# Attention and token/channel MLP on one core: the vector loads, the spread over partitions and some transposes of the first batches done in another way

## The chip, the cores and the metric

The kernel runs on one core of one Trainium2 chip. The metric is the device time of one execution in microseconds. The core has five engines that this text names: PE (TensorE, matrix products and transposes), DVE (VectorE), ACT (ScalarE), POOL (GpSimd) and SP (SyncE, which here only issues DMA transfers). Each engine works through its own list of instructions in a fixed order and waits on semaphores for the others. Data move between the main memory and the on-chip memory by DMA; transfers issued by SP and ACT are described by hardware, those issued by POOL by software (the page calls the queues hardware_dynamic and software_dynamic).

## The reference

Grouped-query attention, and then a residual MLP over tokens and channels with affine layers in place of normalisation. There are 8 batches, 16 query heads on 4 key heads, 384 positions, head size 64 (so 1024 channels).

```python
scores = scale * np.matmul(q, k.transpose(0, 1, 3, 2))      # k, v repeated 4 times over the heads
attn = softmax(scores)
x = np.matmul(attn, v)                                      # as (batch, 384, 1024)
a1 = alpha1 * x + beta1
tok = np.einsum('ts,bsd->btd', w_tok, a1)
u = x + lam * tok
a2 = alpha2 * u + beta2
ch = np.maximum(a2 @ w_ch1, 0.0) @ w_ch2                    # 1024 -> 4096 -> 1024
out = u + lam * ch
```

## The kernel before

The eight batches run one after the other through two stages. The *side* of a batch is everything up to a2: scores, exponentials, AV (attention times v, `av_piece`), the first affine layer, the token product (`tok`), and the transpose of a2 to channels-by-tokens (`a2_transpose`). The *main* part of a batch is the two channel products: `h` (line 408; 32 groups of 8 matmuls, the result goes through bias and relu on ACT or DVE into `hT`) and `ch` (line 435; 6 groups of 32 matmuls). The side of batch b+1 is woven into the main part of batch b: `side` returns a list of small steps, and the loop at the end hands them out by the share of main's matmuls already done. All instruction orders are fixed when the program is built; nothing is rearranged later.

The first batch has nothing to be woven into. Its side is written out by hand: 18 score steps (`scores(i)`), and the table `at` (lines 377 to 383) says what follows each of them. DVE and ACT instructions are issued along with the PE work that feeds them, in the same order. This first stage lasts from 0 to about 42 us; main of the first batch begins there with matmuls of line 152, which belong to chunks 0 and 1.

In it, scale vectors are wanted in three forms. alpha1 times lam (`g1`) is wanted along the free axis in all partitions: the rows lie as 8 rows of 128 in `rows_f`, `scale_rows` (line 512) multiplies alpha1 and beta1 by lam, and `spread_g1` (line 328) spreads each row to 128 partitions by fp32 matmuls with a column of the identity. For the other vectors, `split` (lines 520 to 524) makes a sum of three bf16 parts of each row, and `spread` (line 319) spreads them with bf16 matmuls that add the parts up. alpha2 and beta2 are also wanted with channels on partitions (`al2T`, `be2`): two DMA loads of single elements (line 486). `rows_r` (line 307) makes the sums of w_tok's rows, which with `fill_h` carry beta1 through the token product.

Transposes: in the first two batches k and q are turned by PE, in later ones by DMA (`flip_k`, `flip_q`, issued by SP at 85% of the batch before). The first batch's u is turned in fp32 by PE and scaled by alpha2 in ACT's copy (line 278). For batch 1 (`pe_flip`) a2 is turned by PE (line 288) and copied by ACT (line 291); for batches 2 to 7 SP issues a DMA transpose (line 282). SP also issues the output stores (line 442).

First-layer weights come in 16 chunks of 512 KB a batch, each of them for two groups of `h`, through a ring of five buffers (`load_w1`, line 128, issued by POOL once PE has read the chunk five before). The second-layer weights are loaded once, half of them after the first batch's inputs, and the rest in pieces between the chunks of the first batch (`load_w2`, line 133). All of these go through the software queue in their order of issue.

POOL's order at the start is: the q loads and w_tok, its own copy of v into bf16 (line 536, waits for v), two chunks, the copies of k's second half (line 101), three chunks, a copy of beta2 (line 542), then the inputs of batch 1.

Of the kernel before, what the change touches and what calls it, by code (L numbers as in the profile page):

```python
# [12 lines left out]
def kernel(  # L13
# [21 lines left out]
    nc = tc.nc  # L35
    f32 = mybir.dt.float32
# [3 lines left out]
    MUL = mybir.AluOpType.mult  # L40
    ADD = mybir.AluOpType.add

    B, Hq, S, D = q.shape
# [4 lines left out]
    P = 128  # L48
    NST = S // P
    NDT = DM // P  # L50
    NNT = DFF // P
    NDW = DM // 512
    NP = Hq // 2
# [3 lines left out]
    RING = 5  # L57
# [6 lines left out]
    psum = ST(tc.psum_pool(name="psum", bufs=2))  # L64
# [13 lines left out]
    wtokT = const.tile([P, NST, S], bf, tag="wtokT", name="wtokT")  # L78
# [79 lines left out]
    def side(b):  # L158
# [113 lines left out]
        def a2_transpose(p):  # L272
            if first:
                ps = psum.tile([P, NST, P], f32, tag="tp" if p % 2 else "av", name="ut", bufs=1)
                for tt in range(NST):
                    nc.tensor.matmul(out=ps[:, tt, :], lhsT=x[:, tt, cols(p)], rhs=ident_f, is_transpose=True,  # L276
                                     start=(tt == 0), stop=(tt == NST - 1), skip_group_check=True)
                nc.scalar.activation(out=a2T[:, p, :S], in_=ps.rearrange("p a b -> p (a b)"),
                                     func=mybir.ActivationFunctionType.Copy, scale=al2T[:, p:p + 1])
                return  # L280
            if not pe_flip:
                nc.sync.dma_start_transpose(
                    out=a2T[:, p, :S].rearrange("p (a s) -> p a s", a=NST),
                    in_=a2s[p].rearrange("p a d -> p (a d)"))
# [17 lines left out]


        def rows_r(tag):
            ps = psum.tile([P, S], f32, tag=tag, name="r", bufs=1)
            for st in range(NST):
                nc.tensor.matmul(out=ps[:32], lhsT=ones, rhs=wtokT[:, st, :], start=(st == 0),
                                 stop=(st == NST - 1))
            t = hTf[:32, 10240:10240 + S]
            nc.vector.tensor_copy(out=t, in_=ps[:32])  # L310
            nc.vector.scalar_tensor_tensor(out=R[:32], in0=t, scalar=masks[2], in1=ps[:32], op0=MUL, op1=ADD)


        def spread(ps_, vs, tag, eng="DVE"):
# [3 lines left out]
            for i, p in enumerate(ps_):  # L318
# [6 lines left out]
        def spread_g1(ps_, tag):  # L325
            ps = psum.tile([P, 4, P], f32, tag=tag, name="vec", bufs=1)
            for i, p in enumerate(ps_):
                nc.tensor.matmul(out=ps[:, i], lhsT=ident_f[:NP, p:p + 1].to_broadcast([NP, P]),
                                 rhs=rows_f[:NP, :P], start=True, stop=True)
            nc.vector.tensor_copy(out=g1[:, ps_[0] * P:(ps_[-1] + 1) * P], in_=ps.rearrange("p n d -> p (n d)"))  # L330

        us = []

# [50 lines left out]
        for i in range(18):  # L384
            add(scores, i)
            for f, *a in at.get(i, []):
# [61 lines left out]
    with tc.manual_schedule(engines=order):  # L448
# [9 lines left out]
        load_k(0, [0])  # L458

        hTf = hT.rearrange("p n s -> p (n s)")  # L460
        rows_f = hTf[:32, 9216:10240].bitcast(f32)
        rows_t = hTf[:32, 10240:11264].bitcast(f32)
        rows_b = hTf[:, 11264:11776]
# [4 lines left out]
        be2, al2T = stage[:, 2112:2120], stage[:, 2856:2864]  # L468
        ident_f = hTf[:, 11776:12032].bitcast(f32)
# [5 lines left out]
        sel = stage[:, 2852:2856].bitcast(bf)  # L475
        for t in (stage[:, 2120:2824], rows_b, sel):
            nc.vector.memset(t, 0.0)
        nc.sync.dma_start(out=vst, in_=v[0].rearrange("h (p st) d -> p h st d", st=NST))
# [31 lines left out]
        def scale_rows():  # L510
            r = rows_f[:, :2 * P].rearrange("p (v d) -> p v d", v=2)
            nc.vector.tensor_tensor(out=r, in0=r, in1=rows_f[:, None, 3 * P:].to_broadcast([32, 2, P]), op=MUL)


        def split(lo, hi, step=None):
# [94 lines left out]
```

## Time and profile before

| | |
|---|---|
| median of 3 runs | 815.74 us (813.95 to 815.9) |
| the profiled execution | 814.52 us, its span on the core 812.6 us |
| PE busy | 800.2 us (98%) |
| DVE, ACT, POOL busy | 342.9, 228.1, 179.1 us |
| granted PE clock, mean | 0.996 |
| software DMA queue | 83.28 MB, 82.2% of the 16 DMA engines' time |
| hardware DMA queue of SP | 28.00 MB, 14.1% |

A profile is one execution. Busy PE time is modelled from the starts of pipelined matmuls, so that "98%" says that PE seldom waits, not that it is at its peak. A row such as `L328 PE MATMUL vec<-hT` names the line, the engine, the operation, and what is written from what. The name `hT` also stands for the vectors' rows, and `stage` for v, q and w_tok of the first batch, since these lie in buffers that are used for something else later.

### The profile page before, as it was taken

How to read it: one execution, taken by the hardware profiler on the slowest of the kernel's cores; microseconds unless marked ns; L12 is line 12 of the kernel's file. 1: busy time of each engine (PE TensorE's matmuls, PEld its weight loads, DVE VectorE, ACT ScalarE, POOL GpSimd, SP SyncE). 2: the span in 40 equal slices, each digit the busy share in tenths (PEclk: the TensorE clock that was granted, in tenths of full speed). 3: DMA queues.
4: the chain of work that ended last, by engine and by line, in shares of the span. 5: the costliest groups of instructions: out<-in, count | busy, mean ns of one | idle time of the engine just before them, and what ended most of it. 6: DMA issues, size and time to landing. Idle time of an engine off the chain costs nothing.

```text
span 812.6 us, 14143 instructions
## 1 busy us (share of the span) xinstructions
PE 800.2 (98%) x6098; PEld 453.1 (56%) x6152; DVE 342.9 (42%) x663; ACT 228.1 (28%) x315; POOL 179.1 (22%) x234
## 2 busy tenths in 40 slices
PE   8999999999999999999999999999999999999997
PEld 4766555665456655566455654556555565456545
DVE  6654544244433444334452444424444344442122
ACT  5654421432113321233103331034211432102100
POOL 6144330324003330123301341022500321003000
PEclk8999999999999999999999999999999999999999
DMA  9999997999159992799847997499944999129611
GB/s 198 198 184 200 203 212 133 175 173 175 38 134 178 180 137 66 138 180 175 114 96 131 172 177 90 113 140 176 173 70 100 158 167 132 37 65 183 92 40 40
DMA packets 232111, 112.58 MB, mean 139 GB/s; under 512 B 81009, under 2 KB 225905, under 8 KB 232049
## 3 DMA queue, kind: packets, MB, share of 16 engines
q0 software_dynamic: 169200, 83.28, 82.2%
q1 hardware_dynamic: 62304, 28.00, 14.1%
q8 instruction: 48, 0.79, 0.4%
q10 hardware_dynamic: 544, 0.39, 0.2%
q14 instruction: 15, 0.11, 0.0%
HBM read 170.53 MB, written 12.58 MB: 225 GB/s over the span
## 4 chain that ended last, share of the span: by engine, by line
PE 93%; DVE 3%; DMA 2%; issue 1%; SPq 0%; ACT 0%; DVEq 0%
PE ch L435 41%; PE h L408 37%; PE av L237 4%; PE sc L202 4%; PE tok L259 4%; DMA w<-in_moe_w_ch_dram 2%; DMA hT<-in_moe_lam_dram 1%; DVE hT L418 1%; PE h L152 1%; DVE x L243 1%; DVE a1f L250 0%; DVE a L252 0%; PE ut L276 0%; SPq L481 0%; DVE hT L521 0%
## 5 line engine op out<-in xcount | busy, mean ns | idle before, releaser
L408 PE MATMUL h<-a2T,w 128*128 128x384 bf16 (+1 forms) x2016 | 349.7, 326 | 1.0 <-DVE hT L418 0.3
L435 PE MATMUL ch<-w,hT 128*128 128x512 bf16 (+2 forms) x1546 | 346.1, 370 | 4.4 <-issue 1.0
L408 PEld LDWEIGHTS <-w 128*128 128x128 bf16 x2016 | 189.3, 98 | 125.6 <-issue 8.7
L128 POOL DMA_DIRECT2D w<-in_moe_w_ch_dram x128 | 112.4, 878 | 544.4 <-PE h L408 502.7
L435 PEld LDWEIGHTS <-hT 128*128 128x128 bf16 x1600 | 146.1, 98 | 153.0 <-issue 5.8
L211 ACT ACTIVATE es<-sc 128x1024 bf16<-128x1024 f32 x126 | 123.4, 1021 | 283.4 <-PE sc L202 283.4
L418 DVE TENSOR_SCALAR hT<-h,bias 128x384 bf16<-128x384 f32 x128 | 79.0, 617 | 187.1 <-PE h L408 186.5
L416 ACT ACTIVATE hT<-h,bias 128x384 bf16<-128x384 f32 x128 | 74.3, 581 | 202.9 <-PE h L408 202.4
L440 DVE TENSOR_TENSOR o<-ch,vecs 128x512 f32<-128x512 f32 (+2 forms) x50 | 33.3, 667 | 91.1 <-PE ch L435 91.1
L266 DVE TENSOR_TENSOR x<-tok,x 128x384 f32<-128x384 f32 x64 | 35.5, 555 | 81.3 <-PE tok L259 78.5
L237 PEld LDWEIGHTS <-es 128*128 128x128 bf16 x1008 | 45.8, 97 | 20.5
L237 PE MATMUL av<-v,es 128*128 128x65 bf16 x1008 | 49.0, 193 | 0.0
L202 PE MATMUL sc<-qT,kT 64*128 64x384 bf16 (+2 forms) x576 | 46.2, 275 | 0.1
L259 PEld LDWEIGHTS <-wtokT 128*128 128x128 bf16 x576 | 37.8, 98 | 12.4 <-issue 0.6
L242 DVE RECIPROCAL rinv<-av 128x6 f32<-128x6 f32 x64 | 12.3, 193 | 72.6 <-PE av L237 72.5
L259 PE MATMUL tok<-a,wtokT 128*128 128x128 bf16 x504 | 37.3, 219 | 0.0
L243 DVE TENSOR_TENSOR x<-av,rinv 128x384 f32<-128x384 f32 x64 | 35.7, 557 | 2.2
L202 PEld LDWEIGHTS <-kT 64*128 64x128 bf16 x576 | 19.9, 94 | 28.6 <-issue 24.2
L441 DVE TENSOR_TENSOR o<-o,x 128x512 f32<-128x512 f32 (+2 forms) x50 | 33.5, 671 | 1.7
L270 DVE TENSOR_TENSOR a<-x,vecs 128x384 bf16<-128x384 f32 x56 | 31.8, 569 | 1.9
L252 DVE TENSOR_TENSOR a<-a1f,vecs 128x384 bf16<-128x384 f32 x56 | 31.2, 558 | 2.2
L250 DVE TENSOR_TENSOR a1f<-x,vecs 128x384 f32<-128x384 f32 x56 | 31.2, 558 | 1.9
(75 smaller groups left out, 206.0 us busy)
## 6 DMA issues: line engine op xcount, KB each, us to landing
w<-in_moe_w_ch_dram POOLq DMA_DIRECT2D x135, 512.0 KB, 7.8
out_dram<-o SPq DMA_DIRECT2D x47, 256.0 KB, 2.0
q_raw<-in_q_dram POOLq DMA_DIRECT2D x28, 192.0 KB, 7.1
kst<-in_k_dram SPq DMA_DIRECT2D x16, 192.0 KB, 2.9
w<-in_moe_w_ch_dram POOLq DMA_DIRECT2D x10, 256.0 KB, 12.0
w<-in_moe_w_ch_dram POOLq DMA_DIRECT2D x1, 2048.0 KB, 15.3
v<-in_v_dram POOLq DMA_DIRECT2D x21, 64.0 KB, 6.9
a2T<-a SPq DMA_TRANSPOSE x48, 3.2
```

Source lines behind the costliest of these rows:

```text
L128: nc.gpsimd.dma_start(out=t, in_=w1src[:, :, c * CW * P:(c + 1) * CW * P])
L202: nc.tensor.matmul(out=sc[:, hh, k % 4:k % 4 + n], lhsT=kT[r, sk, 2 * p // G, :], rhs=qT[r, p, st:st + n, :], start=True, stop=True)
L211: nc.scalar.activation(out=e, in_=sc, func=EXP, scale=scale_qk)
L237: nc.tensor.matmul(out=av[:, hh, sq, :], lhsT=ess[k // 4][:, m % 2, k % 4, :], rhs=vb[:, sk, hk, :], start=(sk == 0), stop=(sk == NST - 1))
L243: nc.vector.tensor_tensor(out=x[:, :, cols(p)].rearrange("p st (h d) -> p h st d", h=2), in0=av[:, :, :, :D], in1=rinv.to_broadcast([P, 2, ...
L259: nc.tensor.matmul(out=ps[:, tt, :], lhsT=wtokT[:, st, tt * P:(tt + 1) * P], rhs=a1s[p][:, st, :], start=(st == 0), stop=(st == NST - 1 an ...
L266: nc.vector.tensor_tensor(out=u, in0=ps, in1=u, op=ADD)
L408: nc.tensor.matmul(out=ps[:, :n], lhsT=w1[:, dt, j * P:(j + 1) * P], rhs=a2T[:, dt, :n], start=(dt == 0), stop=(dt == NDT - 1))
L416: nc.scalar.activation(out=hT[:, nt, :], in_=ps[:, :S], func=RELU, bias=c1)
L418: nc.vector.tensor_scalar(out=hT[:, nt, :], in0=ps[:, :S], scalar1=c1, scalar2=0.0, op0=ADD, op1=mybir.AluOpType.max)
L435: nc.tensor.matmul(out=ps[:, lo:hi], lhsT=hT[:, nt, ms * P:(ms + 1) * P], rhs=w2[:, nt, dw * 512 + lo:dw * 512 + hi], start=(nt == 0), sto ...
L441: nc.vector.tensor_tensor(out=o[:, lo:hi], in0=o[:, lo:hi], in1=x[:, ms, c], op=ADD)
```

## The change

- SP's loads at the start: alpha1 and lam now go ahead of v; beta1, alpha2 and beta2 follow after the second part of k, all as rows. The two loads of single elements are gone.
- alpha1 and beta1 are scaled by lam one at a time; alpha1 goes through `split` and the bf16 `spread` (`spread_g1` is gone), beta1's scaling and split come later, at step 6.
- alpha2 and beta2 are turned to channels on partitions by two small PE transposes within `rows_r`, and copied out by DVE. POOL's copy of beta2 is gone.
- The table `at` is laid out anew: the first AV comes after step 5 instead of step 4, most later ones and the token products one step later too; one warm-up matmul after step 3; `rows_r` after step 8.
- POOL issues all five weight chunks ahead of the copies of k's second half.
- Batch 1: the first six of its eight a2 transposes are DMA transposes issued by SP.

```diff
-            if not pe_flip:
+            if not pe_flip or p < 6:
                 nc.sync.dma_start_transpose(
                     out=a2T[:, p, :S].rearrange("p (a s) -> p a s", a=NST),
                     in_=a2s[p].rearrange("p a d -> p (a d)"))
...
         def rows_r(tag):
-            ps = psum.tile([P, S], f32, tag=tag, name="r", bufs=1)
+            ps = psum.tile([P, 512], f32, tag=tag, name="r", bufs=1)
...
+            turned = ps[:, S:S + 2 * NP].rearrange("p (i n) -> p i n", i=2)
+            for i, c in enumerate((2, 4)):
+                nc.tensor.matmul(out=turned[:, i], lhsT=rows_f[:NP, c * P:(c + 1) * P], rhs=ident_f[:NP, :NP],
+                                 is_transpose=True, start=True, stop=True, skip_group_check=True)
...
+            nc.vector.tensor_copy(out=al2T, in_=turned[:, 0])
+            nc.vector.tensor_copy(out=a2T[:, :, S:S + 1], in_=turned[:, 1, :, None])
...
-        at = {0: [(warmup, 3)], 1: [(k_transpose, 1, 1), (scale_rows,), (split, 1, 2, 0)],
-              2: [(q_transpose, 2, 2, "av"), (split, 1, 2, 1)],
-              3: [(spread_g1, lower, "tp")], 4: [(wtok_transpose, 0, "av"), (av, 0), (wtok_transpose, 1, "tp")],
-              5: [(wtok_transpose, 2, "av"), (fill_h, 0), (k_transpose, 2)], 6: [(av, 1), (rows_r, "av")],
-              7: [(q_transpose, 4, 2)], 8: [(av, 2), (fill_h, 4)], 9: [(spread_g1, upper, "tp")], 10: [(tok, 0), (av, 3)],
-              11: [(tok, 1), (q_transpose, 6, 2)], 12: [(ut, 0), (tok, 2)], 13: [(av, 4), (tok, 3)], 14: [(ut, 1), (ut, 2)],
-              15: [(av, 5), (ut, 3)], 16: [(tok, 4)], 17: [(av, 6), (tok, 5)]}
+        at = {0: [(warmup, 3)], 1: [(k_transpose, 1, 1), (scale_rows, 0), (split, 0, 1, 0)],
+              2: [(q_transpose, 2, 2, "av"), (split, 0, 1, 1)], 3: [(warmup, 1)],
+              4: [(spread, lower, (0, 1), "tp"), (wtok_transpose, 0, "av")], 5: [(av, 0), (wtok_transpose, 1, "tp")],
+              6: [(wtok_transpose, 2, "av"), (scale_rows, 1), (split, 1, 2), (k_transpose, 2)],
+              7: [(av, 1), (q_transpose, 4, 2, "av")], 8: [(rows_r, "tp"), (fill_h, 0)],
+              9: [(av, 2), (spread, upper, (0, 1), "av")], 10: [(q_transpose, 6, 2), (tok, 0), (fill_h, 4)],
+              11: [(av, 3)], 12: [(tok, 1), (ut, 0)], 13: [(av, 4), (tok, 2)], 14: [(ut, 1), (tok, 3)],
+              15: [(av, 5), (ut, 2)], 16: [(tok, 4), (ut, 3)], 17: [(av, 6), (tok, 5)]}
...
+        load_row(0, moe_alpha1)
+        load_row(3, moe_lam)
         nc.sync.dma_start(out=vst, in_=v[0].rearrange("h (p st) d -> p h st d", st=NST))
-
-        for i, ap in enumerate((moe_alpha1, moe_beta1, moe_alpha2, moe_lam)):
-            nc.sync.dma_start(out=rows_f[:, i * P:(i + 1) * P],
-                              in_=bass.AP(tensor=ap.tensor, offset=ap.offset, ap=[[0, 4], [P, NP], [1, P]]))
         load_k(0, [2])
-        with nc.allow_non_contiguous_dma(reason="one small vector, once"):
-            for t, ap in ((al2T, moe_alpha2), (be2, moe_beta2)):
-                nc.sync.dma_start(out=t, in_=ap.rearrange("(dt di) -> di dt", di=P))
+        load_row(1, moe_beta1)
+        load_row(2, moe_alpha2)
+        load_row(4, moe_beta2, 1)
...
-        load_w1(0)
-        load_w1(1)
+        for c in range(RING):
+            load_w1(c)
         place_k(0, 1)
-        for c in range(2, RING):
-            load_w1(c)
-        nc.gpsimd.tensor_copy(out=a2Ts[0][:, :, S:S + 1], in_=be2[:, :, None])
```

`load_row(i, ap, n=4)` loads a vector as 8 rows of 128 into columns i of `rows_f`, n times below each other.

More of the change, by code (lines that the diff above doesn't have):

```diff
@@ L304, in rows_r @@
         def rows_r(tag):
-            ps = psum.tile([P, S], f32, tag=tag, name="r", bufs=1)
+            ps = psum.tile([P, 512], f32, tag=tag, name="r", bufs=1)
             for st in range(NST):
-                nc.tensor.matmul(out=ps[:32], lhsT=ones, rhs=wtokT[:, st, :], start=(st == 0),
+                nc.tensor.matmul(out=ps[:32, :S], lhsT=ones, rhs=wtokT[:, st, :], start=(st == 0),
                                  stop=(st == NST - 1))
-            t = hTf[:32, 10240:10240 + S]
-            nc.vector.tensor_copy(out=t, in_=ps[:32])
-            nc.vector.scalar_tensor_tensor(out=R[:32], in0=t, scalar=masks[2], in1=ps[:32], op0=MUL, op1=ADD)
+            turned = ps[:, S:S + 2 * NP].rearrange("p (i n) -> p i n", i=2)
+            for i, c in enumerate((2, 4)):
+                nc.tensor.matmul(out=turned[:, i], lhsT=rows_f[:NP, c * P:(c + 1) * P], rhs=ident_f[:NP, :NP],
+                                 is_transpose=True, start=True, stop=True, skip_group_check=True)
+            t = hTf[:32, 10496:10496 + S]
+            nc.vector.tensor_copy(out=t, in_=ps[:32, :S])
+            nc.vector.scalar_tensor_tensor(out=R[:32], in0=t, scalar=masks[2], in1=ps[:32, :S], op0=MUL, op1=ADD)
+            nc.vector.tensor_copy(out=al2T, in_=turned[:, 0])
+            nc.vector.tensor_copy(out=a2T[:, :, S:S + 1], in_=turned[:, 1, :, None])
         def spread(ps_, vs, tag, eng="DVE"):
@@ L322, in spread @@
                       in_=ps[:, :n * w].rearrange("p (n v) d -> p n v d", n=n))
[L325 to L330, printed above, removed]
         us = []
@@ L460 @@
         hTf = hT.rearrange("p n s -> p (n s)")
-        rows_f = hTf[:32, 9216:10240].bitcast(f32)
-        rows_t = hTf[:32, 10240:11264].bitcast(f32)
-        rows_b = hTf[:, 11264:11776]
+        rows_f = hTf[:32, 9216:10496].bitcast(f32)
+        rows_t = hTf[:32, 10496:11520].bitcast(f32)
+        rows_b = hTf[:, 11520:12032]
         stage = sb.tile([P, NST * DM], f32, tag="x", name="stage", bufs=2)
@@ L467 @@
         wtok_in = stage[:, 1536:2112].bitcast(bf).rearrange("p (tt s) -> p tt s", tt=NST)
-        be2, al2T = stage[:, 2112:2120], stage[:, 2856:2864]
-        ident_f = hTf[:, 11776:12032].bitcast(f32)
+        al2T = stage[:, 2112:2112 + NDT]
+        ident_f = hTf[:, 12032:12288].bitcast(f32)
         R = stage[:, 2120:2312].bitcast(bf)
@@ L477, with load_row @@
             nc.vector.memset(t, 0.0)
+        def load_row(i, ap, n=4):
+            nc.sync.dma_start(out=rows_f[:n * NP, i * P:(i + 1) * P],
+                              in_=bass.AP(tensor=ap.tensor, offset=ap.offset, ap=[[0, n], [P, NP], [1, P]]))
+        load_row(0, moe_alpha1)
+        load_row(3, moe_lam)
         nc.sync.dma_start(out=vst, in_=v[0].rearrange("h (p st) d -> p h st d", st=NST))
-        for i, ap in enumerate((moe_alpha1, moe_beta1, moe_alpha2, moe_lam)):
-            nc.sync.dma_start(out=rows_f[:, i * P:(i + 1) * P],
-                              in_=bass.AP(tensor=ap.tensor, offset=ap.offset, ap=[[0, 4], [P, NP], [1, P]]))
         load_k(0, [2])
-        with nc.allow_non_contiguous_dma(reason="one small vector, once"):
-            for t, ap in ((al2T, moe_alpha2), (be2, moe_beta2)):
-                nc.sync.dma_start(out=t, in_=ap.rearrange("(dt di) -> di dt", di=P))
+        load_row(1, moe_beta1)
+        load_row(2, moe_alpha2)
+        load_row(4, moe_beta2, 1)
         for h in (0, 2):
@@ L507, with scale_rows @@
                 nc.vector.tensor_reduce(out=t[:n], in_=ident[:n, :n].rearrange("p (k c) -> p c k", c=NP), op=ADD, axis=AX)
-        def scale_rows():
-            r = rows_f[:, :2 * P].rearrange("p (v d) -> p v d", v=2)
-            nc.vector.tensor_tensor(out=r, in0=r, in1=rows_f[:, None, 3 * P:].to_broadcast([32, 2, P]), op=MUL)
+        def scale_rows(i):
+            r = rows_f[:, i * P:(i + 1) * P]
+            nc.vector.tensor_tensor(out=r, in0=r, in1=rows_f[:, 3 * P:4 * P], op=MUL)
         def split(lo, hi, step=None):
```

## The prediction

> **What bounds the kernel now.** I read the page first, then the chain, the tensor engine's waits, the stages, and the landing of each weight chunk.
>
> ```profile
> PE 800.2 (98%) x6098; PEld 453.1 (56%) x6152; DVE 342.9 (42%) x663; ACT 228.1 (28%) x315; POOL 179.1 (22%) x234
> ...
> DMA  9999997999159992799847997499944999129611
> ```
>
> TensorE is busy for 98% of the span, so a change pays only in PE work removed or in one of the few PE waits. The DMA row is full in the first slices, some 120 us. Part 4, the chain, in order of time:
>
> ```profile
> 3.98 5.84 DMA hT<-in_moe_lam_dram
> ...
> 73.09 13.36 DMA w<-in_moe_w_ch_dram
> 86.45 0.05 issue
> 86.50 1.48 PE h L408 x8
> ```
>
> The first line is the load that the change targets. The others tell more: the last first-layer weight chunk of the first batch (chunk 15) is issued at 73.09, lands at 86.45 and is used at 86.50. PE's waits in the first 100 us (total, times, longest):
>
> ```profile
> PE vec L328 <- PE sc L202: 0.9, 1, 0.9
> PE tp L188 <- DMA stage<-in_q_dram: 0.6, 1, 0.6
> PE tp L177 <- DVE wtokT L300: 0.4, 1, 0.4
> PE tp L297 <- DVE vecs L330: 0.3, 1, 0.3
> PE h L408 <- DVE hT L418: 0.3, 1, 0.3
> ```
>
> The 0.9 us is the fp32 spread; the chain puts lam and L512 behind it. The stages (PE busy with count, PEld, DVE, ACT, POOL, granted clock, DMA share, GB/s):
>
> ```profile
> 9.20:12.59 3.39, 2.50 (x37) 1.92 (x37) 2.50 (x8) 2.40 (x3) 1.51 (x3) 1.00 1.64 173
> 12.59:19.41 6.82, 6.14 (x57) 3.37 (x52) 5.52 (x15) 2.80 (x4) 5.27 (x8) 0.50 1.41 213
> 46.00:86.00 40.00, 39.63 (x346) 24.64 (x345) 20.04 (x47) 21.84 (x40) 18.42 (x24) 1.00 1.38 198
> 41.00:45.50 4.50, 4.48 (x33) 2.69 (x31) 2.71 (x9) 3.02 (x8) 1.97 (x3) 1.00 0.80 152
> 10.00:12.00 2.00, 1.53 (x15) 1.23 (x16) 1.90 (x6) 1.01 (x3) 0.92 (x3) 1.00 1.71 147
> 185.00:187.50 2.50, 2.50 (x25) 1.57 (x23) 1.82 (x4) 0.31 (x1) 0.88 (x1) 1.00 1.77 121
> ```
>
> PE runs at half clock from 12.59 to 19.41. From 46 to 86 the DMA engines carry 198 GB/s without a break, and PE loses its lead over the weights: chunk 5 lands at 48.9 and is used at 52.3 (lead 3.4 us), chunk 10 leads by 1.4, 13 by 1.1, 14 by 0.5, 15 by 0.05. A chunk with its second-layer piece takes 3.95 us to move, PE's work on it 3.2 to 3.5. So this stage is bound by DMA at its end: an earlier PE waits for chunk 15.
>
> **The Trainium skill.** "TensorE: Matmul & The Clock Gate", What's actually happening: the clock halves after an idle window of about 3.4 us, and windows run free of the kernel. The trace agrees on length (6.83 us, two windows), but it halved after a window 74% busy (2.50 of 3.39). "DMA: Bandwidth & Descriptors", Why small descriptors are slow: each packet has a fixed cost. Here the element loads of alpha2 and beta2 (2,048 packets of 4 bytes) fall into 10 to 12, where the rate is 147 against 195 just after. The same page, Issuing engines are not separate DMA queues: all transfers share 16 engines. The row 185.00 shows it: during one DMA transpose the rate falls to 121.
>
> **The change, part by part.**
>
> *First batch, early (7 to 42 us).* Removed: two fp32 spreads, 16 matmuls (8 in groups of 1.08 us), 2.16 us of PE. Added: two bf16 spreads at 0.22 (row L319, four of 128x128), one warm-up (0.17), and two small fp32 transposes, not in the trace: 0.06 each (floor, their moving side is 8 wide) to 0.14 (the ut row, 0.41 for three), I take 0.1. PE net: -2.16 + 0.44 + 0.17 + 0.20 = -1.35. On DVE the split of beta1 moves up from work with alpha1 to its own five instructions (0.21, 0.21, 0.34, 0.21, 0.40, 0.24 with its scale: about 1.7 us) ahead of the k copy, plus two 8-wide copies at 0.15 (row L414). SP issues alpha1 and lam second and third, so DVE's first scale waits for its k copy's end (8.74) rather than 9.95. v is issued at about 2.8 instead of 1.25: it landed 5.1 after its issue; at the same pace 7.9, with fewer bytes ahead 7.2. POOL waits there; five weight issues (0.88 each) now stand before the k copies, which end at about 7.2 + 0.83 + 4.4 + 0.96 = 13.4, against 12.04. k's transposes are due after 13.4 in both orders: covered by the second token-weight copy (L300). AV a step later covers v. Two new waits: SP holds alpha2's row until the first k load has landed (issued 0.74, DVE reads it at 4.12) and beta2's until alpha1's has; behind them stand only batch 1's k loads, not needed before 40. PE's two small transposes wait for these rows at about step 8 (18 us), where in the old order the element loads had landed by 15.4; behind them PE's scores, but the rows are 10 us early. ACT's scaled copies now wait for DVE's copy of alpha2 (about 20) rather than a DMA, and are first due at 25: hidden. POOL loses its wait of 0.8 us for beta2 and a copy (0.35, L542), ahead of batch 1's q loads, which have 15 us to spare: nothing.
>
> Laying DVE, ACT and PE rows end to end in the old order, with half clock in its place, gives 42.0 for the end of the early stage; the trace has 42.06. In the new order: 39.7 at full clock, 40.7 with the same half window. With v at 10: 40.9 and 42.1. So PE comes 1.3 to 2.4 us earlier to chunk 2.
>
> *What stops it.* The DMA stream up to chunk 15 has the same bytes. It gains (a) the element loads' cost: (195 - 147) x 2 / 195 = 0.5 us; (b) the dip at 41 to 45.5, which comes because chunk 5's load waits for PE to free chunk 0: (205 - 152) x 4.5 / 205 = 1.2 us, filled if PE is 1.2 us or more earlier. Sum 1.7.
>
> *Batch 1's flips.* Six of eight transposes leave PE: 3 matmuls, 0.17 us each in the chain; ACT loses six copies of 0.48 (L291), worth nothing, as ACT is 28% busy. One (86.11) is before chunk 15, where the wait swallows it; five after (95.3 to 125.4): 5 x 0.167 = 0.83 us gained. SP gains six DMA transposes:
>
> ```profile
> L282 SPq DMA_TRANSPOSE a2T<-a x48: 1177/1185/1832, 171.7 to 720.3; - x48
> ...
> DMA to landing us min/median/max: 2.3/3.2/7.5
> ```
>
> Each holds SP for 1.18 us, in the order p0, p1, out 1, p2, out 2, p3, out 3, p4, out 4, p5, the k and q flips of batch 2. Output stores behind them are 8 us apart, with four buffers. The q flip (issued 129.3, median landing 6.6, first needed at 140.84) has 4.9 us to spare; p5 costs it 1.2. Its q rows land at 126.5; four transposes at 1 us each less the 1.7 put that at 129. Hidden. The pieces of w2's second half land by 112.9, wanted from 118.3 on: hidden too.
>
> p0 isn't. It follows the first tok (77.4, DVE done 79.2) and moves 3 us later, while chunks 14 and 15 are in flight. Its price in a full stage: in 185.0 to 187.5 the software queue moved 413 packets, against 375/us in the quiet stretch before (5.0 us at 191 GB/s): 1.4 us lost; in 272.5 to 274, 349 packets: 0.6; in 175.5 to 178, 456: 1.1. I take 1.0.
>
> Chunk 15 lands 1.7 - 1.0 = 0.7 us earlier. Sum: 0.7 + 0.8 = **1.5 us gained**. From the profiled execution (814.52, span 812.6) that is 813.0; the median of the runs is 1.2 above it, so **814.2** against 815.74. About 0.3% (2.4 us) is what a measurement of this kernel can tell from no change: this lies inside.
>
> Bounds: gain (b) half reached and p0 at 1.4: 0.5 + 0.6 - 1.4 + 0.8 = 0.5. p0 at 0.6: 1.9; p0 outside the stage: 2.5.
>
> **Rivals.**
>
> *B: the early gain reaches the end.* If the transpose costs the weight queue little, or chunks come faster, 1.3 to 2.4 plus 0.83 to 1.0: 2.1 to 3.4, middle 2.8, so 812.9. For it: PE is on the chain nearly everywhere. Against: the lead of 0.05 us at chunk 15.
>
> *C: half clock in the paced stage (slower).* Waiting for chunks 13 to 15 makes PE 81% busy (3.2 of 3.95), and 74% was halved before. Place: 75 to 90. Price: 6.83 us at half is 3.4 lost, so one window ends at 814.2 + 3.4 = 817.6, inside 0.3%; from the second window on it decides: 817.6 + 3.4 = 821 less what the waits absorb (0.75 x 2), some 819.5. Against: dense matmuls fill these chunks; 46 to 86 ran at 1.00.
>
> *D: early stage not shorter.* v or the k copies come late (v at 10), PE reaches chunk 2 as before. Only the flips are left: 0.8, less up to 0.9 as p0 now delays chunk 15: 815 to 815.8.
>
> **Chances.** A (forecast) 0.55, B 0.22, C 0.11, D 0.12. A's own spread 812.9 to 815.7. Faster by over 0.3% (below 813.3): most of B and a tenth of A, 0.23; slower: C's upper part and scatter, 0.09; within: 0.68. Range 8 in 10: from B's middle and the scatter of the runs (1.95 us) 812.0, to C's first window 817.0.
>
> **What would show it.** The scale of alpha1 starts before 9 us; no fp32 spread; early stage ends at 39.5 to 41; no dip at 41 to 45; PE waits of 0.3 to 0.8 us for weight DMAs before chunks 12 to 15, chunk 15 used at about 85.8; p0's packets between 79 and 84 with the rate near 120; PE then without gaps, 0.83 us less work to 140. Wrong if chunk 15 is used before 84.8 (B), the clock shows 0.5 after 46 (C), the early stage ends after 41.7 (D), or the first scores of batch 2 wait for the q flip.

## The result and the profile after

The changed kernel takes 815.2 us (median of 4 runs, 814.74 to 817.27) beside 815.49 us for the kernel before (4 runs on the same chip): the ratio is 1.0005, interval 0.9983 to 1.0027. Measured again with 15 runs beside 43 (experiment e10), the ratio is 1.0017, interval 1.0008 to 1.0026, some 1.4 us more than before. The time lies in the range and within 0.3%, as forecast; but the gain of 1.5 us isn't there, and rival D (early stage not shorter) is what the trace shows. The profiled execution took 814.84 us with a span of 813.1, against 814.52 and 812.6.

The page of the changed kernel, the tensor engine's row and the row of the DMA engines' load:

```profile
PE 797.7 (98%) x6076; PEld 449.7 (55%) x6129; DVE 345.8 (43%) x671; ACT 225.2 (28%) x309; POOL 178.7 (22%) x233
...
DMA  9999999999169992799947997499945999129611
```

PE has 2.5 us less to do (797.7 against 800.2), and the time doesn't fall. The chain in order of time says what the work is waiting for instead (start, duration, what):

```profile
2.81 7.16 DMA stage<-in_v_dram
9.97 0.06 issue
10.03 0.90 POOL v L538
10.93 4.38 POOL w L128 x5
15.31 1.04 POOL k L101 x2
16.35 0.05 issue
16.40 0.51 PE tp L177 x6
...
73.16 0.72 issue
73.88 13.75 DMA w<-in_moe_w_ch_dram
87.68 1.48 PE h L407 x8
```

The chain used to begin with lam's row and DVE. Now it begins with v: its load, POOL's copy of it, POOL's five weight issues and k's copies stand in one row, and PE's transposes of k's second half wait at their end. Chunk 15 is still what PE waits for later: it lands at 87.63 and is used at 87.68, where before it was 86.45 and 86.50. PE's waits in the first 100 us (total, times, longest):

```profile
PE tp L177 <- POOL k L101: 2.7, 1, 2.7
PE warm L452 <- DVE wtokT L455: 1.5, 1, 1.5
PE vec L325 <- DVE hT L526: 0.8, 1, 0.8
PE tok L259 <- DVE x L266: 0.8, 2, 0.6
PE h L407 <- DMA w<-in_moe_w_ch_dram: 0.6, 1, 0.6
```

The wait of 0.9 us for the fp32 spread (L328) is gone, and 0.8 us at its successor L325 stands in its place: the bf16 spread waits for DVE's split. The first row is new, 2.7 us. POOL's timeline shows its cause; the brackets give POOL's idle time before the copy and what ended it, v's load:

```profile
10.03 0.90 POOL L538 CAST v<-stage 128x768 bf16<-128x768 f32 x1 [5.24 <-DMA stage<-in_v_dram]
10.88 4.43 POOL L128 DMA_DIRECT2D w<-in_moe_w_ch_dram  x5
15.26 1.08 POOL L101 CAST k<-kst 128x384 bf16<-128x384 f32 x2
```

The stages (window, length, PE busy with count, PEld, DVE, ACT, POOL, granted clock, DMA share, GB/s):

```profile
10.90:13.50 2.60, 2.13 (x39) 1.51 (x38) 1.87 (x6) 2.10 (x4) 2.60 (x4) 1.00 0.71 102
14.33:17.74 3.41, 1.34 (x29) 1.03 (x30) 3.01 (x9) 0.60 (x2) 3.41 (x6) 1.00 1.41 192
17.74:21.16 3.42, 3.42 (x29) 1.59 (x26) 2.43 (x6) 1.72 (x3) 2.05 (x4) 0.50 1.40 199
41.00:45.50 4.50, 4.49 (x29) 2.62 (x28) 2.78 (x10) 3.09 (x8) 1.75 (x2) 1.00 1.05 203
46.00:86.00 40.00, 39.69 (x348) 24.67 (x346) 20.05 (x48) 21.55 (x40) 19.13 (x24) 1.00 1.39 198
```

For the kernel before, the first of these windows:

```profile
10.90:13.50 2.60, 2.29 (x37) 1.65 (x37) 2.50 (x9) 1.09 (x2) 2.42 (x4) 0.82 1.58 176
```

Three things are to be seen. From 10.9 to 13.5 only 102 GB/s move, against 176: POOL waited for v until 10.03 and then copied it, the first weight chunk was issued at 10.88 instead of 7.16, and the weight queue ran dry. In the window 14.33 to 17.74 PE is busy for 1.34 of 3.41 us, and the next window runs at half clock. And the dip is gone from the stretch 41 to 45.5 (203 against 152 GB/s; from 42 to 46 it is 183 against 160), though the early stage ends later: chunk 2 is first used at 43.05, against 42.21. The stream is late by then, so that it still has work while PE frees the next buffer; e1 and e2 below test this reading from both sides.

The transposes that SP issues in batch 1 (duration on SP, then issue to landing):

```profile
L282 SPq DMA_TRANSPOSE a2T<-a x6: 1185/1236/1282, 80.0 to 128.0; - x6
...
DMA to landing us min/median/max: 6.2/6.8/7.3
```

From chunk 15's use to chunk 16's (the first of batch 1's main part) it takes 52.75 us instead of 53.59. So the account is: chunk 5 lands 0.51 us later (49.37 against 48.86), chunk 15 is used 1.18 later, chunk 16 0.34 later, and the execution takes 0.32 us longer. From the use of chunk 16 to the end it is 672.5 to 672.7 us in all fourteen traces of this study, so that the difference between two kernels is made before it.

### The profile page after: what moved, and what is told of

It is laid out like the page before. It is cut to its first block, busy times and chain, and to the rows that moved or that the text cites. A ratio compares the mean times of both kernels' runs of the same rounds, so it can differ in the third digit from the quotient of the medians.

```text
span 813.1 us, 14108 instructions
## 1 busy us (share of the span) xinstructions
PE 797.7 (98%) x6076; PEld 449.7 (55%) x6129; DVE 345.8 (43%) x671; ACT 225.2 (28%) x309; POOL 178.7 (22%) x233
## 4 chain that ended last, share of the span: by engine, by line
PE 92%; DVE 4%; DMA 3%; issue 1%; POOL 1%; SPq 0%; ACT 0%; DVEq 0%
PE ch L434 41%; PE h L407 37%; PE av L237 4%; PE sc L202 4%; PE tok L259 4%; DMA w<-in_moe_w_ch_dram 2%; DMA stage<-in_v_dram 1%; DVE hT L417 1%; DVE x L243 1%; PE h L152 1%; POOL w L128 1%; DVE a1f L250 0%; DVE a L252 0%; PE ut L276 0%; DVE rinv L242 0%
```

## The experiments

The theory after the result (V): v's late landing holds POOL, and through POOL both the weight queue and k's copies. Its rivals: the DMA transpose of block 0 takes the gain (called T in the expectations); the new order on PE and DVE is no shorter in itself (P); the delay is k's copies alone (an order on POOL, whatever v does); or it is PE's clock. Ratios are times against the kernel before, with 95% intervals; the kernel before had medians of 814.87, 814.66, 814.58 and 814.64 us in the four groups of runs (e1 to e4, e6 to e9, e10 to e12, e13).

### e1: v's load ahead of the rows again

```diff
+        nc.sync.dma_start(out=vst, in_=v[0].rearrange("h (p st) d -> p h st d", st=NST))
         load_row(0, moe_alpha1)
         load_row(3, moe_lam)
-        nc.sync.dma_start(out=vst, in_=v[0].rearrange("h (p st) d -> p h st d", st=NST))
```

> The changed kernel with v loaded ahead of the rows of alpha1 and lam again (one line moved). Theory V (v's late landing, at 9.97 us, costs the early gain twice: POOL's k copies come late and PE waits 2.7 us for them, and the weight queue, whose first chunk POOL issues after v's copy, runs dry from 11 to 13.5, so that every chunk lands later): v lands at 6.3 to 6.6, the first chunk is issued at about 7.3, PE's wait for the k copies is under 0.5 us, the early stage ends at 39.7 to 41, chunk 15 is used at 85.3 to 86.2, and the time is 1.5 to 2.3 us under the changed kernel. Theory T (the DMA transpose of batch 1's first a2 block, which moves while chunk 15 is in flight, sets the end by itself): chunk 15 is used within 0.4 us of 87.7 whatever the early stage does, time as the changed kernel. Theory P (the new order of PE and DVE is no shorter in itself): v lands early, but the early stage still ends at 42.5 or later.

Measured: 815.04 us, ratio 1.0006 (0.9995 to 1.0016). The means work: v lands at 6.39, the first chunk is issued at 7.21, k's copies are done at about 12.6, and the queue isn't dry. The windows of this kernel:

```profile
6.72:10.13 3.41, 3.41 (x21) 1.09 (x19) 0.77 (x2) 1.67 (x2) 3.41 (x5) 1.00 1.30 216
...
10.90:13.50 2.60, 1.53 (x16) 0.85 (x13) 2.02 (x7) 2.39 (x3) 2.60 (x5) 1.00 1.42 212
...
42.00:46.00 4.00, 3.98 (x30) 2.39 (x28) 2.30 (x7) 2.69 (x8) 1.80 (x3) 1.00 0.61 126
```

The end doesn't follow: the forecast of 1.5 us or more below the changed kernel is missed. What came is the sign named for theory P, and chunk 15 is used at 88.12, later than in the changed kernel. In this trace DVE's scale of alpha1 starts at 10.19 instead of 8.75, and the early stage ends at 42.88. In this execution that isn't the rows' later place: DVE waits for its k copy, and that one for PE, whose first products ran slower until 10.13 (0.61 us for a group of four score products that takes 0.39 afterwards; the record of the tensor clock begins with full speed at 10.13). In e11, which also has v first, the scale starts at 8.68. The groups on DVE of this kernel, from the copy to the end of the split:

```profile
9.91 0.36 DVE L179 COPY kT<-tp 128x384 bf16<-128x384 bf16 x1 [2.03 <-PE tp L177]
10.19 0.27 DVE L514 TENSOR_TENSOR hT<-hT 32x128 f32<-32x128 f32 x1
...
12.75 0.21 DVE L526 CAST hT<-hT 32x128 bf16<-32x128 f32 x1
```

So 2.8 us pass on DVE from the scale to the spread's operands, where the old spread needed the scale alone. The old early part, begun as slowly, loses nothing here: e12 (below) has its first full speed at 9.78, and its fp32 spread starts at 10.77 without a wait. The new one in e1, and the old one in e12 as far as the view goes (to 11 us):

```profile
13.02 0.38 PE L325 MATMUL vec<-hT,stage 128*128 128x128 bf16 x4 [0.79 <-DVE hT L526]
...
10.77 0.48 PE L328 MATMUL vec<-hT 8*128 8x128 f32 x2
```

A stream that is early and a PE that is late then give the deepest dip of all traces, 126 GB/s from 42 to 46. That explains this one execution. Whether the other twelve began as slowly isn't on record, so why e1 is no faster than the kernel before stays open.

### e2: k's copies after two chunks, as in the kernel before

```diff
-        for c in range(RING):
-            load_w1(c)
+        load_w1(0)
+        load_w1(1)
         place_k(0, 1)
+        for c in range(2, RING):
+            load_w1(c)
```

> The changed kernel with POOL's copies of k's second half ahead of weight chunks 2 to 4, as in the kernel before. v still lands late. If PE's 2.7 us wait for the k copies is what counts: time 1.5 us or more under the changed kernel. Theory V in full (the weight queue's delay counts as well): PE's wait falls to 0.5 us or less, the early stage ends about 1.5 us earlier (41.0 to 41.6), but chunk 15 still lands at 87.2 to 87.8, PE waits 1.5 to 2.5 us for chunks 12 to 15 instead of 0.6, and the time is within 0.4 us of the changed kernel.

Measured: 814.03 us, 0.9993 (0.9985 to 1.0002). PE's waits for k and for the weights:

```profile
PE tp L177 <- POOL k L101: 1.5, 1, 1.5
PE h L407 <- DMA w<-in_moe_w_ch_dram: 1.2, 1, 1.2
```

The early stage ends at 41.22, the queue is still dry (112 GB/s in 10.9 to 13.5), and chunk 15 is used at 86.40, not at the 87.2 to 87.8 that theory V in full named. The late stream meets an early PE, and what it lacked by 14 us it has again by 50 (see the table at the end):

```profile
42.00:46.00 4.00, 3.97 (x33) 2.52 (x30) 3.75 (x12) 1.56 (x5) 2.67 (x4) 1.00 1.27 241
```

So the place of k's copies is a part of the cost, the dry queue isn't needed for that part, and what a dry queue loses early need not be lost at the end.

### e3: block 0 of batch 1 turned by PE

```diff
-            if not pe_flip or p < 6:
+            if not pe_flip or 0 < p < 6:
```

> The changed kernel with blocks 1 to 5 of batch 1's a2 turned by DMA and block 0 by PE again. Theory T, and the price taken in the prediction: chunk 15 lands 0.6 to 1.0 us earlier (86.6 to 87.1), PE's wait of 0.6 us before it goes, and PE's transpose costs 0.17 back: time 0.3 to 0.5 us under the changed kernel. If block 0's transfer did not delay the chunk: chunk 15 lands at 87.6 as before, time the same.

Measured: 814.74 us, 1.0002 (0.9994 to 1.0010). In its profiled execution the wait for k's copies was 3.9 us, the early stage ended at 43.65 and one chunk interval was 4.74 us, so its trace doesn't compare with the other by the end (chunk 15 lands at 88.50, not at the forecast's 86.6 to 87.1). The interval from chunk 14's landing to chunk 15's does: 3.89 us, against 4.57. The DMA transpose is not where the gain went: without it the kernel is as fast as the kernel before, not faster.

### e4: the early part alone, batch 1 as before

```diff
-            if not pe_flip or p < 6:
+            if not pe_flip:
```

> The changed kernel with all of batch 1's a2 blocks turned by PE as in the kernel before: the early part of the change alone. As the prediction priced the flips: five transposes of 0.17 us come back after chunk 15, block 0's stands before it in place of 0.4 to 0.6 us of waiting; time 0.3 to 0.6 us over the changed kernel, 0.8 to 1.0 us over the kernel before, with chunk 15 used at 86.9 to 87.3.

Measured: 815.88 us, 1.0012 (1.0005 to 1.0020): the new early part costs 1.0 us by itself. The chain has the same head:

```profile
2.82 6.71 DMA stage<-in_v_dram
9.58 0.83 POOL v L538
10.41 4.34 POOL w L128 x5
14.75 1.06 POOL k L101 x2
```

### e6: two chunks ahead of POOL's copy of v

```diff
+        load_w1(0)
+        load_w1(1)
         nc.gpsimd.tensor_copy(out=vt[0][:, :, :, :D], in_=vst.rearrange("p h st d -> p st h d"))
-        for c in range(RING):
+        for c in range(2, RING):
             load_w1(c)
         place_k(0, 1)
```

> The changed kernel with weight chunks 0 and 1 issued by POOL ahead of v's copy (so they don't wait for v); the k copies still come after all five chunks. Theory V, its weight-queue half alone: the rate no longer falls between 11 and 13.5 (195 GB/s or more), the first half of w2 lands at 43.0 to 43.6 instead of 44.8, PE's wait for the k copies falls from 2.7 to about 0.9 us because only three issues stand ahead of them, the early stage ends near 41.2, the dip at 41 to 45 is gone, chunk 15 lands at 85.2 to 86.4; time 1.0 to 2.2 us under the changed kernel. If the queue running dry did not count: chunk 15 lands at 87 or later and the time stays within 0.5 us.

Measured: 813.95 us, 0.9989 (0.9983 to 0.9996). v is as late as in the changed kernel (landing at 9.70), but the queue is fed; k's copies are at 13.25 and PE still waits 2.0 us for them:

```profile
10.90:13.50 2.60, 1.42 (x28) 0.94 (x28) 2.35 (x8) 2.12 (x3) 2.60 (x4) 1.00 1.41 212
```

212 GB/s in place of 102, and the kernel is 0.16% faster than the first measurement of the changed one, 0.28% than the second. v's lateness as such is therefore not the cost: it is what POOL had queued behind v. (e1, in which nothing on POOL is held up either and which is still no faster, is the run that this leaves unexplained.) In the profiled execution, though, chunk 15 lands at 87.27 instead of the 85.2 to 86.4 expected, and PE's wait for k's copies is 2.0 us instead of 0.9; the gain is in the runs, and this trace doesn't show where. The edit isn't wholly pure, as k's copies also stand behind three issues instead of five (13.25 against 15.31), and its interval overlaps e2's: which of the two costs is the larger isn't told.

### e7: e6, and k's copies right after v's

```diff
+        load_w1(0)
+        load_w1(1)
         nc.gpsimd.tensor_copy(out=vt[0][:, :, :, :D], in_=vst.rearrange("p h st d -> p st h d"))
-        for c in range(RING):
-            load_w1(c)
         place_k(0, 1)
+        for c in range(2, RING):
+            load_w1(c)
```

> As e6, and the k copies directly after v's copy, ahead of chunks 2 to 4: neither PE nor the weight queue waits for v. Theory V: no PE wait for the k copies over 0.3 us, early stage ends at 39.7 to 40.9 (clock windows move it), chunk 15 lands at 84.8 to 86.2 with a PE wait of 1 to 2.5 us before chunks 13 to 15, since the stage is bound by DMA; time 1.3 to 2.3 us under the kernel before (ratio 0.9972 to 0.9984). Theory T, that block 0's transfer undoes it: chunk 15 still lands at 87 or later, ratio 0.9995 or more. Theory P: early stage ends after 42.

Measured: 813.34 us, 0.9986 (0.9979 to 0.9993). The time is just above its forecast of 0.9972 to 0.9984. PE's wait for k's copies has become one of 1.0 us for DVE, which the old early part has in its place too (0.4 in the profile of the kernel before, 0.9 to 1.0 in e9 and e12), so k is covered:

```profile
PE vec L325 <- DVE hT L526: 1.1, 1, 1.1
PE tp L177 <- DVE wtokT L300: 1.0, 1, 1.0
```

Here the dip at 41 to 45.5 is back (179 GB/s), with the early stage done at 41.15 and chunk 15 used at 85.63, the forecast's 85.8.

### e8: e7 without the DMA transpose of block 0

The edit of e7 and that of e3 together.

> As e7, with block 0 of batch 1's a2 turned by PE. If block 0's DMA transpose costs chunk 15 the 0.6 us that the gap between landings shows: chunk 15 lands 0.5 to 0.7 us earlier than in e7, PE gets 0.17 us back, and the time is 0.3 to 0.6 us under e7 (ratio to the kernel before 0.9965 to 0.998). If it costs nothing: as e7 or 0.1 us slower.

Measured: 812.82 us (21 runs), 0.9980 (0.9973 to 0.9986): faster than both kernels. It is 0.5 us below e7, which agrees with 0.64 us for block 0 (see e9 and e12), but the two intervals overlap. Its trace misses the forecast for chunk 15: it lands at 86.31, after e7's 85.59, behind a half window and an interval of 5.06 us between chunks 13 and 14.

### e9 and e12: the kernel before with the flips alone

e9 turns blocks 1 to 5 by DMA, e12 blocks 0 to 5; the early part is the old one.

```diff
-            if not pe_flip:
+            if not pe_flip or 0 < p < 6:    # e9;  e12: p < 6
```

> The kernel before with blocks 1 to 5 of batch 1's a2 turned by DMA, nothing else. As the prediction priced the flips: PE loses five transposes of 0.17 us after chunk 15, early stage and chunk 15 as before (42.1; 86.5), no wait for the q flip of batch 2: 0.7 to 0.9 us under the kernel before (ratio 0.9989 to 0.9991). If the output stores or the flips behind them on SP's queue are held up to harm: time the same or over.

> The kernel before with all six blocks of batch 1 turned by DMA. Blocks 1 to 5 alone gave 0.9991. If the transpose of block 0 costs the paced weight stream 0.6 to 1.0 us and chunk 15's landing sets the end, this gives back most of it: 0.9997 to 1.0003, and chunk 15 is used 0.6 to 1.0 us after the 86.0 of that run. If the transpose is hidden, 0.9990 to 0.9992 and chunk 15 at 86.0.

Measured: e9 814.08 us, 0.9991 (0.9983 to 0.9999); e12 814.25 us, 0.9999 (0.9991 to 1.0008). In e9 chunk 15 to chunk 16 takes 52.75 us, 0.84 less than before. e12's ratio is 0.0008 higher, 0.65 us, though again the intervals overlap. The chains:

```profile
72.34 13.59 DMA w<-in_moe_w_ch_dram
85.98 1.48 PE h L408 x8
```

for e9, and for e12:

```profile
71.92 13.90 DMA w<-in_moe_w_ch_dram
85.86 1.48 PE h L408 x8
```

Chunk 15 is not used 0.6 to 1.0 us after e9's, as was expected of e12: e12's early stage ended at 41.02, e9's at 41.45, and its stream ran ahead by so much. The interval that both traces share tells it: from chunk 14's landing to chunk 15's it is 3.99 us in e9 and 4.54 in e12. Over all traces it is 4.52 to 4.57 where block 0 goes by DMA (eight kernels, mean 4.545) and 3.86 to 3.99 where it goes by PE (six, mean 3.905): 0.64 us is what the transpose takes from the weight stream.

Both also show the old early part twice more: 41.45 and 41.02 for its end, without a half-clock window, where the profile of the kernel before has 42.21 with 6.8 us at half clock.

### e10: the changed kernel again

> The changed kernel as it is, measured again with more executions beside the kernel before. If it is only the sum of the early part alone (1.0012 measured) and the flips alone (0.9991 for five of six, block 0 as yet open), the ratio is 1.0003; a ratio of 0.9990 or below would mean that the flips gain more in the changed kernel than in the old one, and above 1.0010 that they gain less.

Measured: 815.88 us (15 runs), 1.0017 (1.0008 to 1.0026). The 1.0003 of the expectation is missed; the sum of the parts with e12 in e9's place, 1.0012 and 0.9999, lies within this interval. Its trace has the same picture, more strongly: the wait for k's copies is 3.9 us, and two neighbouring windows read

```profile
12.59:16.00 3.41, 0.02 (x1) 0.00 (x0) 3.24 (x9) 0.87 (x1) 3.41 (x6) 1.00 1.23 147
16.00:19.42 3.42, 2.91 (x34) 2.24 (x34) 1.43 (x5) 1.02 (x1) 3.39 (x5) 0.50 1.44 193
```

PE idles through the first, and the second runs at half clock.

### e11: e8 with v first on SP

The edit of e8 and that of e1 together.

> The changed kernel with two weight chunks ahead of POOL's copy of v, k's copies ahead of the other three, block 0 turned by PE, and v's load ahead of the rows of alpha1 and lam on SP. If v's late landing still costs the weight stream or PE something in the fastest version (ratio 0.9980), v first makes it 0.3 to 1 us faster: 0.9968 to 0.9976. If POOL's order has already taken away what v's lateness costs, and DVE's chain behind lam gets longer instead, it is equal or up to 0.5 us slower: 0.9980 to 0.9986.

Measured: 813.22 us, 0.9989 (0.9982 to 0.9996). Not faster than e8, and above the 0.9986 that was named for no gain, though the intervals overlap. Once POOL's order no longer hangs on v, v first on SP's list brings nothing; whether it costs something, as e1 too would allow, was not tested by itself. Its profiled execution has the earliest chunk 15 of all (landed 85.17), so one trace would have called it the best.

### e13: PE's wait for k filled with idle products

The 13 products compute nothing that is used.

```diff
-              6: [(wtok_transpose, 2, "av"), (scale_rows, 1), (split, 1, 2), (k_transpose, 2)],
+              6: [(wtok_transpose, 2, "av"), (scale_rows, 1), (split, 1, 2), (warmup, 13), (k_transpose, 2)],
```

> The changed kernel with 13 idle products (0.17 us each, 2.2 us) put on PE just where it waits 2.7 to 3.9 us for POOL's copies of k's second half; k's copies come no earlier. If only the wait itself costs time, this changes nothing or costs a little (ratio to the kernel before 1.0005 to 1.0017, as the changed kernel), and a window of 3.41 us at half clock still follows. If the half window follows because PE idles through most of a 3.41 us window, PE's share in the window ahead rises above the 64% from which no window was halved in most traces, the half window is gone, the early stage ends about 1.7 us x 2.9 / 3.4 = 1.4 us earlier (41.6 to 42.0 instead of 43.05 and 43.35), chunk 15 lands about as much earlier, and the ratio falls by 0.0012 to 0.0018: 0.9990 to 1.0003.

Measured: 814.82 us, 1.0002 (0.9993 to 1.0011), at the upper edge of what the clock theory gives, and with an interval that overlaps the changed kernel's. The windows:

```profile
12.94:16.35 3.41, 2.44 (x20) 1.47 (x17) 3.24 (x9) 1.02 (x1) 3.41 (x6) 1.00 1.31 170
16.35:19.76 3.41, 2.96 (x45) 1.85 (x43) 2.89 (x8) 2.05 (x2) 2.83 (x4) 1.00 1.43 186
```

PE is busy for 2.44 of 3.41 us, and the next window is at full clock. k's transposes start no earlier (16.37), and the early stage ends at 42.21 instead of 43.05 and 43.35. Of chunk 15 the theory fails: it lands at 87.70, as in the changed kernel. The queue was as dry as there (104 GB/s from 10.9 to 13.5), and PE's earlier arrival ended in a wait of 1.2 us for that chunk.

The runs say the same of all executions. Each has its mean granted clock on record, and one window at half clock takes 0.002 from it. A mean of 0.999 or more have 1 of the changed kernel's 19 executions, 13 of e13's 14, and 5 of the 19 of the kernel before beside e13. So the idle products did remove the half window. Yet the median of those 13 is 814.73 us and that of those 5 is 813.58: without any half window e13 is still 1.1 us behind, so the clock is not the whole of the cause. (The changed kernel's one execution without it took 813.70 us; what else was different there isn't on record.)

### The runs side by side

One profiled execution each. "Moved" is what all DMA engines moved from 2 us to 14, to 50 and to 58, the sum of windows of 4 us, each its GB/s times 4. The last column says whether block 0 goes by DMA.

| kernel | moved to 14, KB | to 50 | to 58 | early stage ends | chunk 15 lands | ratio | block 0 |
|---|---|---|---|---|---|---|---|
| before | 2640 | 9612 | 11172 | 42.21 | 86.45 | 1 | PE |
| after | 2456 | 9488 | 11068 | 43.05 | 87.63 | 1.0005 | DMA |
| after, e10 | 2432 | 9408 | 10960 | 43.35 | 87.90 | 1.0017 | DMA |
| e13, wait filled | 2468 | 9600 | 11088 | 42.21 | 87.70 | 1.0002 | DMA |
| e4, no flips | 2552 | 9520 | 11032 | 42.65 | 87.20 | 1.0012 | PE |
| e3, no block 0 | 2408 | 9376 | 10868 | 43.65 | 88.50 | 1.0002 | PE |
| e1, v first | 2832 | 9528 | 11092 | 42.88 | 88.07 | 1.0006 | DMA |
| e2, k earlier | 2428 | 9728 | 11332 | 41.22 | 86.35 | 0.9993 | DMA |
| e6, chunks earlier | 2732 | 9744 | 11224 | 41.38 | 87.27 | 0.9989 | DMA |
| e7, both | 2788 | 9840 | 11420 | 41.15 | 85.59 | 0.9986 | DMA |
| e8, both, no block 0 | 2732 | 9740 | 11332 | 41.51 | 86.31 | 0.9980 | PE |
| e11, e8 with v first | 2816 | 9852 | 11420 | 41.12 | 85.17 | 0.9989 | PE |
| e9, old early part, five flips | 2624 | 9744 | 11328 | 41.45 | 85.93 | 0.9991 | PE |
| e12, old early part, flips | 2632 | 9808 | 11400 | 41.02 | 85.82 | 0.9999 | DMA |

The bytes moved by 58 us order the landings of chunk 15 roughly; from 58 to 82 the distances between the kernels stay as they are, to within 15 KB. At 200 GB/s the changed kernel's 104 KB less are 0.52 us; with 0.64 us for block 0 (see e9 and e12) that makes 1.16, and chunk 15 came 1.18 later. The same sum holds within 0.3 us for eight of the other twelve. It isn't exact: e1, e3, e6 and e8 landed 0.4 to 0.7 us later than it says, and no run explains that.

Two places make the sum: what the queue has lost by 14 us (184 KB in the changed kernel) and the dip around 42 to 50, which depends on when PE arrives and on how far ahead the stream is (126 GB/s from 42 to 46 in e1, 241 in e2). In e13, PE's earlier arrival had made up nearly all of the loss by 50 (12 KB short of the kernel before, the changed kernel 124), but by 58 it was 84 KB short again. With block 0 that is 1.1 of the 1.25 us by which its chunk 15 came later than before. Why e13 fell back between 50 and 58 no run shows.

## Why the prediction came out as it did

**The number: luck.** 814.2 was forecast for a gain of 1.5 us, and 815.2 and 815.88 were measured, without a gain. Both lie in the range, but so does no change at all: the kernel before had medians of 814.58 to 814.87 in the later groups, so that its first median, 815.74 of three runs, was high.

**What bounds the kernel: right.** Chunk 15 is used 0.05 us after its landing in the profiles of before, after and all variants, and what comes after it is PE's work alone.

**The flips after chunk 15: right.** Forecast 0.83 us, measured 0.84 in each trace that has them. The q flip is hidden as forecast: PE's waits up to 150 us show none for it.

**Block 0's transpose: right mechanism, size too large.** Taken 1.0 us, bounds 0.6 and 1.4; it costs 0.64. (One of its three prices was also worked out wrong: 456 packets in the 2.5 us from 175.5, at 375 a microsecond, are 1.3 us lost, not 1.1.)

**v's landing: the step that failed.** "At the same pace 7.9, with fewer bytes ahead 7.2" was taken for a landing that came at 9.97. The load's own 5.1 us was carried over to a place where it has two row loads ahead of it on SP and POOL's queue beside it. In the trace of the changed kernel the first k load's packets of 768 bytes end on SP's queue at about 3.6, the rows' packets of 512 bytes follow from 4.2, and v's begin at about 4.9; in the kernel before, v's packets follow k's without a gap, by 3.5. From issue to landing v took 7.16 us. The bound "v at 10" stood in the prediction and was priced for the end of the early stage (40.9 to 42.1); even that was too low against 43.05. Two things were missing.

- *The cover.* k's copies were put at 13.4, under the second token-weight copy. That cover ends at about 14.3 to 14.6 (in e13 PE's wait for it ends at 14.26; in the changed kernel the first of two such copies starts at 14.23). With v at 10 the same sum, 0.9 + 4.4 + 1.0 us after v, gives 16.3, as measured: nearly 2 us past the cover. The durations were right, and the check of the cover was made for the good case alone.
- *The queue behind the wait.* The prediction named POOL's five issues as ahead of k, not as behind v. They are: v's copy stands first, so the first chunk was issued at 10.88 and the stream lost 184 KB by 14 us. That takes the place of gain (a), 0.5 us, which no longer showed in a queue without work.

**The early stage: 0.84 us longer instead of 1.3 to 2.4 shorter.** To the 2.7 us wait the clock adds: the Trainium skill's "TensorE: Matmul & The Clock Gate", What's actually happening, has the clock halve after an idle window of about 3.4 us. The traces agree on the length (3.41 us), but the window need not be idle: here the wait makes one that is 39% busy in the changed kernel and 1% in e10, and half clock follows both. A window at half clock loses up to 1.7 us. The removed wait for the spread came back too, 0.8 of 0.9 us: the prediction had the scale earlier, and it is (8.75 against 9.95), but between scale and spread now stand the five instructions of the split, which the fp32 spread didn't need. The new spread starts at 11.37, the old one started at 10.47 and was done at 11.59. And the two small transposes took 0.14 us each at full clock (0.28 for two in e13), the upper bound, not 0.1.

**The dip: the sign came, its cause didn't.** "No dip at 41 to 45" was named as evidence for the forecast. It is not there, at 203 GB/s, because the stream arrived late, while PE was late too. Where PE did arrive early beside a timely stream, e12, the rate was 202 GB/s and chunk 15 landed 0.63 us earlier than in the kernel before, in spite of block 0: that gain exists.

**Rivals.** D is what happened, at the place named (v at 10) and near its time, 815 to 815.8. B didn't, C didn't: from 46 to 86 the clock is 1.00. The half window that did come lies in the early stage; the prediction's sums had carried the old one along there, but no case had a new wait bring one. The range's upper end was named after C's first window, which the prediction itself puts at 817.6, not 817.0.

**What would have been enough:** e7 shows the forecast's picture without its flaw: PE waits for DVE only, the early stage ends at 41.15, chunk 15 is used at 85.63, and the ratio is 0.9986, 1.1 us below the kernel before. So a gain near the forecast's was there to be had, with two chunks ahead of v's copy and k's copies ahead of the other three. That it is the forecast's own gain isn't shown. e7 also issues its first chunk at 4.76, where the kernel before does at 7.16, and the kernel before with its chunks so placed was not run. Nor is its early stage shorter than the old one in e9 and e12, 41.45 and 41.02. And 13 of its 17 executions have no half window, against 17 of 61 of the kernel before beside it; among these alone the medians are 813.09 and 813.96, 0.9 us apart.

## What to carry to other kernels

When a load is moved behind others, price its landing again with all that now shares the engines, and follow the engine that waits for it through everything queued behind that wait, DMA issues above all: one wait for v here held the whole weight stream back by 3.7 us (first issue at 10.88 instead of 7.16). Judge each cover at the bad end of the unknown number as well as at the good one. A sign in a trace (a dip that is gone) proves a theory only if the other theory wouldn't show it too.

## What the runs showed of the hardware

- Which windows were halved: in the thirteen traces of this study other than before's, each window of 3.41 us, up to 28 us, with PE busy for 0 to 56% of it was followed by one at half clock (seven), and none with 64% or more was, the lowest being 64 and 65% in e7 and e11. The one exception is the kernel before, halved after 74% and again after 80%. These shares count transposes as busy; whether the hardware does was not tested. Experiment e2 shows the upper end of the halved ones:

```profile
11.82:15.23 3.41, 1.90 (x32) 1.11 (x29) 3.03 (x9) 1.35 (x3) 3.41 (x6) 1.00 0.96 122
15.23:18.65 3.42, 3.42 (x34) 2.00 (x32) 2.73 (x8) 2.00 (x2) 3.42 (x5) 0.50 1.40 197
```

- The profiled early stage of one program ends at different times, with half windows in one execution and none in another: 42.21, 41.45 and 41.02 for the same old early part. A difference below 1 us there isn't told by one trace. Of the 172 executions of the kernel before in the four groups, 52 have a mean granted clock of 0.999 or more and a median of 813.65 us, the other 120 one of 814.98.
- A DMA transpose of 128x384 bf16 in the full weight stream costs that stream 0.64 us and lands after 6.2 to 7.3 us, while its median in the whole kernel is 2.3 us.
